# Attention value products: a head pair's thirty products in two visits instead of four, with the last 64 keys' values kept twice beside rows of zeros

## The chip, the core and the metric

The kernel runs on one core of a Trainium2 chip. The core has a matrix engine (TensorE, PE in the profile; its weight loads are listed apart as PEld), VectorE (DVE), ScalarE (ACT), GpSimd (POOL), and SyncE (SP), which issues most of the DMA transfers. Each engine works through its own queue in order. The metric is the time of one execution on the device, in microseconds; smaller is better. A profiled execution leaves a trace with the start and duration of each instruction.

## What is computed

Eight heads of four batches attend over 576 positions with 64 features per head, after rotary embedding of queries and keys. The result goes through two feed-forward layers with different nonlinearities. Everything is float32.

```python
q_rot, k_rot = rotate(q), rotate(k)                  # 4 x 8 x 576 x 64
scores = matmul(q_rot, k_rot.T) / sqrt(64)           # 576 x 576 per head
attn = exp(scores - max(scores))
attn = attn / (sum(attn) + 1e-9)
x = matmul(attn, v)                                  # heads side by side: 2304 x 512
h = x @ w_in;  x = where(h > 0, h, exp(min(h, 0)) - 1) @ w_out     # first layer
h = x @ w2_in; out = (h - tanh(h)) @ w2_out                        # second layer
```

## The kernel before

Two heads are treated together as a pair; there are 16 pairs. The 576 queries of a head are cut into four blocks of 128 and one of 64; the two blocks of 64 of a pair are put together into one. So a pair has nine **items**: item 0 is the first block of head 0, item 1 the first block of head 1, and so on to item 8, which holds the last 64 queries of both heads.

An item passes through these steps. TensorE makes its scores (`emit_s`, tile `s`, 128 queries by 576 keys; the records of line 212). VectorE takes the row maximum (`emit_max`, line 221). ScalarE takes the exponential with that maximum as bias and adds up the denominator (`emit_exp`, line 235). VectorE inverts the denominators and GpSimd scales both heads' rows (`emit_norm`, lines 248 to 252). TensorE transposes the scaled rows, 128 keys at a time (`emit_t`, tiles `pt` and `pr`, lines 292, 298 and 305). VectorE or ScalarE copies the transposes to SBUF (`flush`, lines 266 and 268), and TensorE multiplies them with the values (`emit_pv`, tile `o`, line 326). ScalarE copies `o` out (line 273).

The value products are grouped by queries: group 0 holds query blocks 0 and 1 (256 columns), group 1 blocks 2 and 3 (256 columns), group 2 the last 64 queries. Each group sums over five chunks of keys, `c` from 0 to 4, and over two heads. Chunks 0 to 3 have 128 keys each: 128 rows of the array and 64 columns. Chunk 4 has the last 64 keys, and both heads' chunks lie in one tile: head 0 in partitions 0 to 63, head 1 in 64 to 127. Their product is made with 64 rows and 64 columns. A float32 value product stands as two records in the trace.

The order is written out by hand in one loop over passes `i`. A pass issues, on TensorE, the scores of item `i+1`, then the transposes of item `i-4`, then the value products that are due; on VectorE the maximum of item `i`, the copies of the transposes made in the pass before, the inverses for item `i-1`, and pieces of the rotary embedding and of the conversion of weights; on ScalarE the exponential of item `i`, copies, and pieces of the same. When value products are due is told by `PV_AT`: for each group and chunk, how many passes after the group's last transposes. A **visit** is one pass in which TensorE makes value products. Counted from a pair's first item, they come in passes 8, 10, 12 and 14. Since pass `i` begins with the scores of item `i+1`, the text below counts **steps**: step r is the time on TensorE from the scores of item r of a pair to those of the next item. Passes 8, 10, 12 and 14 are steps 0 and 2 (of the next pair's count), 4 and 6.

Two tiles hold scores (`ps_s`, `bufs=2`), so the scores of item `n+2` wait for the exponential of item `n`. Three tiles hold transposes, one holds `o`. The keys of a pair are prepared by VectorE (the last piece, line 157, in the pass of item 4 of the pair before) and spread by four DMA transfers that SyncE issues (line 179). The values of a pair are loaded by one DMA (line 134), ten passes before their first use, into one of two tiles. After attention, TensorE does the two layers (lines 448 to 733).

The prediction speaks of the line `PV_AT`, of `load_v` and `emit_pv`, and of the tile `fm`, which holds temporaries of the conversion of weights and of both layers.

Of the kernel before, what the change touches and what calls it, by code (L numbers as in the profile page):

```python
# [8 lines left out]
F32 = mybir.dt.float32  # L9
# [14 lines left out]
def attention_elu_tanhshrink(ctx: ExitStack, tc: tile.TileContext, qk, v, w1i, w1o, w2i, w2o, tab, out):  # L24
# [6 lines left out]
    nc = tc.nc  # L31
    NPAIR = qk.shape[0]
    NTOK, DM = out.shape
    S = 576
    NB = 384
# [6 lines left out]
    const = ctx.enter_context(tc.tile_pool(name="const", bufs=1))  # L42
# [1 line left out]
    xa = const.tile([128, KC * NTOK], F32, name="xa")  # L44
    blk = {i: const.tile([128, 2, 2, NB], F32R, name=f"blk{i}") for i in range(2)}
    wmem = [const.tile([128, 8192], F32R, name="wa")]
    fm = const.tile([128, 6656], F32, name="fm")

    def x_hl(t, part, c):
        return blk[2 * t + c // 2][:, part, c % 2, :]  # L50
# [39 lines left out]
    def split_w(hi, lo, f):  # L90
        nc.scalar.copy(out=hi, in_=f)  # L91
        nc.gpsimd.tensor_tensor(out=lo, in0=f, in1=hi.bitcast(F32), op=ALU.subtract)  # L92
# [16 lines left out]
    with ExitStack() as actx:  # L109
        acst = actx.enter_context(tc.tile_pool(name="acst", bufs=1))  # L110
        p1 = actx.enter_context(tc.tile_pool(name="p1", bufs=1))
        p2 = actx.enter_context(tc.tile_pool(name="p2", bufs=2))
# [9 lines left out]
        qa_t = [acst.tile([128, 640], F32R, name=f"qa{i}") for i in range(2)]  # L122
        qb_t = [acst.tile([128, 640], F32R, name=f"qb{i}") for i in range(2)]

        t_t, hl_t, v_t, k_t = {}, {}, {}, {}

        def load_qk(p, x):
# [2 lines left out]
            t_t[p, x] = t  # L130

        def load_v(p):
            t = p2.tile([128, S], F32, tag="v", name="v")
            nc.sync.dma_start(out=t, in_=v[p])
            v_t[p] = t

        def prep(p, x, i):
            t = t_t[p, x]
# [171 lines left out]
        def emit_pv(p, grp, c):  # L310
            aT, aTr = aT_t[p, grp]
            n = 256 if grp < 2 else 64
            vt = v_t[p]

            if c == 0 and grp < 2:
                o_t[p, grp] = ps_v.tile([128, 512], F32, tag="o", name="o")
            o = o_t[p, min(grp, 1)]
            if grp == 2:
                o = o[:, 256:320]
            for h in range(2):  # L320
                sl = slice(64 * h, 64 * h + 64)
                if c < 4:
                    w, m = vt[:, 128 * c + 64 * h:128 * c + 64 * h + 64], aT[:, h, c, 0:n]
                else:
                    w, m = vt[sl, 512:576], aTr[sl, 0:n]
                nc.tensor.matmul(out=o[sl, 0:n], lhsT=w, rhs=m, start=(c == 0), stop=(c == 4))  # L326
            if c < 4:
                return
            aT_t.pop((p, grp))
            if grp == 2:  # L330
                v_t.pop(p)
            if grp != 1:
                late_x.append((p, min(grp, 1), o_t.pop((p, min(grp, 1))), 256 if grp == 0 else 320))
# [18 lines left out]
        with tc.manual_schedule():  # L352
            for x in range(2):
                t = t_t[0, x] = p2.tile([128, 2, S], F32, tag=f"t{x}", name=f"t{x}")
# [4 lines left out]
            load_qk(1, 0)  # L359
            load_qk(1, 1)  # L360
            load_v(0)
            make_identity(nc, ident)
            nc.vector.memset(zero, 0.0)
            for i in range(2):
                nc.scalar.copy(out=qa_t[i][:, S:640], in_=zero)
                nc.scalar.copy(out=qb_t[i][:, 0:64], in_=zero)
            for i in range(3):
                prep(0, 0, i)
            for i in range(3):
                prep(0, 1, i)  # L370
            n = len(items)
            pend = []
            nw = list(range(len(first_w)))[::-1]
            emit_s(0)
            PV_AT = ((1, 1, 1, 3, 3), (1, 1, 1, 3, 3), (2, 2, 2, 2, 2))
            for i in range(3, 5):
                for x in range(2):
                    prep(0, x, i)
            for i in range(n + D + 1):
                p, r = divmod(i, NI)  # L380
# [22 lines left out]
                if 0 <= i - D < n:  # L403
                    emit_t(i - D)
                    pp, uu, hh = items[i - D]
                    if uu in (1, 3) and hh == 1 or uu == 4:
                        for c in range(5):
                            pend.append((i + PV_AT[uu // 2][c], pp, uu // 2, c))
                for x in [x for x in pend if x[0] <= i]:
                    emit_pv(*x[1:])  # L410
                    pend.remove(x)
                if n - 8 <= i < n and (i - n) % 2 == 0:
                    split_x(0, (i - n + 8) // 2)
            while pend:
                emit_pv(*pend.pop(0)[1:])
# [3 lines left out]
    fcst = ctx.enter_context(tc.tile_pool(name="fcst", bufs=1))  # L419
# [6 lines left out]
    for i in range(2, 2 * NT):  # L426
        blk[i] = fcst.tile([128, 2, 2, NB], F32R, name=f"blk{i}")
    wmem.append(fcst.tile([128, 8192], F32R, name="wb"))
    gt3 = fcst.tile([128, 3, 2, NB], F32R, name="gt3")
    acc = xa  # L430
    b1 = fcst.tile([128, 1], F32, name="b1")
# [6 lines left out]
    n = len(steps)  # L438
# [13 lines left out]
        h_t[i] = hp  # L452

    def emit_act(i):
        f = fm[:, 5376 + NB * (i % 3):5376 + NB * (i % 3) + NB]
        nc.scalar.activation(out=f, in_=h_t[i], func=AF.Relu, scale=-1.0)  # L456
        nc.scalar.activation(out=f, in_=f, func=AF.Exp, scale=-1.0)
        f_t[i] = f
# [62 lines left out]
    nst, staged = [0], []  # L521

    def stage_out(cols, dst):
        st = fm[:, 4352 + 512 * (nst[0] % 2):4864 + 512 * (nst[0] % 2)][:, 0:cols.stop - cols.start]
        nst[0] += 1
        split_w(st.bitcast(F32R), GM[:, cols].bitcast(F32R), GM[:, cols])
        staged.append((dst, st, GM[:, cols]))
# [54 lines left out]
    def x2(t, k):  # L582
        return xa.rearrange("p (c n) -> p c n", n=NTOK)[:, 2 * k:2 * k + 2, NB * t:NB * t + NB]

    tms = [fm[:, o:o + 2 * NB].rearrange("p (a n) -> p a n", a=2) for o in (0, 5760, 5760)]
    XORD = ("B11", "B21", "T2", "T1", "T3", "T4", "B22")
    xb = {(tp, nm): blk[(7 * tp + k) % 8] for tp in range(NT // 2) for k, nm in enumerate(XORD)}

# [43 lines left out]
    def tmp(tag, bufs):  # L632
        base = {"s": 0, "h22": 6, "u": 7, "w": 9, "mask": 11, "f": 13}[tag]
        k = tmp_n.get(tag, 0)
        tmp_n[tag] = k + 1
        o = NB * (base + k % bufs)
        return fm[:, o:o + NB]

    LAG = 4
    with tc.manual_schedule():  # L640
# [146 lines left out]
        for q in range(nq + 1):  # L787
            live = q < nq
            p = q - 1
# [19 lines left out]
            if live:  # L809
                b, c, a, spare = banks  # L810
# [125 lines left out]
```

## Time and profile before

| | us |
|---|---|
| three runs, lowest, median, highest | 1108.22, 1108.41, 1108.49 |
| the profiled execution, its own time | 1107.93 |
| span of its trace | 1106.1 |
| TensorE busy in it | 1067.5 |
| fourteen head pairs, pair 1's first scores to pair 15's | 254.57 |

The span runs from the first instruction to the last; 1.8 us of the execution lie around it. Attention takes up the first 318 us. An engine's busy time is the time in which one of its instructions was under way, and TensorE's instructions overlap: the end of one is modelled and lies after the start of the next. So how long a group of TensorE records really holds the engine is read from start to start, not from the durations.

### The profile page before, as it was taken

The page shows a single profiled execution, that of the slowest core. Times are in us where ns is not written, and L with a number is a line of the kernel's source. Part 1 is how long each engine was busy: PE and PEld are TensorE (multiplying, and loading weights), DVE is VectorE, ACT ScalarE, POOL GpSimd, SP SyncE. Part 2 cuts the span into 40 slices and gives each one's busy share as a digit, 9 for nine tenths or more (in the row PEclk, how much of TensorE's full clock was granted, in tenths as well). Part 3 has the DMA queues.
Part 4 walks back from the last instruction along what each step waited for, and adds up shares of the span by engine and source line. Part 5 has one row for each costly group of instructions (what it writes and reads, how often), then busy time and mean ns, then how long its engine had stood idle before and what let it go on. Part 6 is the DMA issues. An engine that isn't in the chain of part 4 may idle for free.

```text
span 1106.1 us, 18779 instructions
## 1 busy us (share of the span) xinstructions
PE 1067.5 (97%) x6512; PEld 955.2 (86%) x6512; DVE 756.5 (68%) x1435; ACT 725.5 (66%) x1562; POOL 695.8 (63%) x648
## 2 busy tenths in 40 slices
PE   2999999999999999999999999999999999999998
PEld 1777776777779999999999999988998989888986
DVE  6888888888735555675766765376767667865674
ACT  2676766676757765555555555588777876878672
POOL 2877887888549766555465565556576556655552
PEclk9999999999999999999999999999999999999999
DMA  7777676767304354344443764255446754556431
GB/s 235 220 202 192 182 206 186 200 179 221 80 20 143 100 179 140 106 153 168 134 137 103 251 224 147 93 191 184 165 161 212 259 187 168 191 156 231 173 127 57
DMA packets 83390, 184.27 MB, mean 167 GB/s; under 512 B 8032, under 2 KB 43872, under 8 KB 83296
## 3 DMA queue, kind: packets, MB, share of 16 engines
q1 hardware_dynamic: 75520, 154.76, 44.2%
q10 hardware_dynamic: 7776, 28.32, 8.7%
q8 instruction: 52, 0.85, 0.3%
q14 instruction: 42, 0.34, 0.1%
HBM read 126.94 MB, written 27.79 MB: 140 GB/s over the span
## 4 chain that ended last, share of the span: by engine, by line
PE 78%; DVE 8%; POOL 5%; ACT 4%; DMA 2%; issue 2%; SPq 0%; ACTq 0%; POOLq 0%; DVEq 0%
PE y L505 18%; PE h L448 18%; PE yb L698 14%; PE hb L733 8%; PE o L326 7%; PE s L212 5%; PE pt L292 3%; PE cvb L733 3%; DVE nm L221 2%; POOL a L252 1%; ACT a L235 1%; DVE fm L766 1%; DVE t L149 1%; DMA v<-in_v 1%; DMA t<-in_qk 1%
## 5 line engine op out<-in xcount | busy, mean ns | idle before, releaser
L252 POOL TENSOR_SCALAR a<-a,r 128x576 f32<-128x576 f32 x144 | 135.6, 954 | 63.2 <-DVE r L249 43.2
L489 POOL TENSOR_TENSOR gt<-fm,gt 128x384 fp32r<-128x384 f32 x119 | 123.4, 1037 | 76.5 <-ACT gt L488 68.8
L235 ACT ACTIVATE a<-s,nm 128x576 f32<-128x576 f32 x144 | 107.0, 743 | 89.0 <-DVE nm L221 74.7
L698 PE MATMUL yb<-wb,blk 128*128 128x512 f32 x603 | 154.3, 392 | 0.4 <-POOL blk L489 0.4
L733 PE MATMUL hb<-blk,wa 128*128 128x384 f32 x720 | 139.9, 337 | 2.0 <-DVE fm L766 2.0
L221 DVE TENSOR_REDUCE nm<-s 128x1 f32<-128x576 f32 x144 | 108.2, 753 | 38.2 <-PE s L212 36.6
L733 PEld LDWEIGHTS hb<-blk,wa 128*128 128x128 f32 x720 | 127.1, 188 | 7.3 <-DVE fm L766 3.0
L698 PEld LDWEIGHTS yb<-wb,blk 128*128 128x128 f32 x603 | 112.5, 188 | 22.6 <-POOL blk L489 0.8
L456 ACT ACTIVATE fm<-h 128x384 f32<-128x384 f32 x96 | 47.3, 493 | 124.8 <-PE h L448 108.0
L489 POOL TENSOR_TENSOR blk<-fm,blk 128x384 fp32r<-128x384 f32 x67 | 71.3, 1065 | 87.8 <-ACT blk L488 59.4
L448 PE MATMUL h<-blk,wa 128*128 128x384 f32 x576 | 107.8, 335 | 0.8 <-POOL blk L55 0.6
L505 PE MATMUL y<-gt,wa 128*128 128x384 f32 x576 | 107.6, 334 | 0.1
L505 PE MATMUL y<-gt,wb 128*128 128x384 f32 x576 | 107.6, 334 | 0.0
L448 PE MATMUL h<-blk,wb 128*128 128x384 f32 x576 | 107.6, 334 | 0.0
L473 DVE TENSOR_SCALAR cvb<-fm 128x512 f32<-128x512 f32 x56 | 38.9, 694 | 98.6 <-ACT fm L471 96.0
L448 PEld LDWEIGHTS h<-blk,wa 128*128 128x128 f32 x576 | 100.3, 188 | 1.8 <-POOL blk L55 0.9
L505 PEld LDWEIGHTS y<-gt,wa 128*128 128x128 f32 x576 | 100.5, 188 | 0.4 <-issue 0.4
L505 PEld LDWEIGHTS y<-gt,wb 128*128 128x128 f32 x576 | 100.5, 188 | 0.0
L448 PEld LDWEIGHTS h<-blk,wb 128*128 128x128 f32 x576 | 100.5, 188 | 0.0
L92 POOL TENSOR_TENSOR fm<-fm 128x512 fp32r<-128x512 f32 (+1 forms) x48 | 58.4, 1220 | 57.0 <-ACT fm L91 55.8
L326 PE MATMUL o<-aT,v 128*64 128x256 f32 (+1 forms) x768 | 89.6, 338 | 2.8 <-ACT aT L268 2.4
L147 POOL TENSOR_TENSOR t<-t,tabs 128x576 f32<-128x576 f32 x59 | 86.2, 1462 | 7.9 <-DMA t<-in_qk 7.9
(124 smaller groups left out, 2281.5 us busy)
## 6 DMA issues: line engine op xcount, KB each, us to landing
wa<-wi SPq DMA_DIRECT2D x96, 448.0 KB, 5.1
wb<-wo SPq DMA_DIRECT2D x48, 512.0 KB, 6.3
k<-hl SPq DMA_DIRECT2D x64, 288.0 KB, 4.4
t<-in_qk SPq DMA_DIRECT2D x30, 576.0 KB, 6.1
wi<-fm SPq DMA_DIRECT2D x48, 256.0 KB, 2.0
fm<-in_w2o ACTq DMA_DIRECT2D x16, 512.0 KB, 3.8
wo<-fm SPq DMA_DIRECT2D x32, 256.0 KB, 3.2
fm<-in_w2i ACTq DMA_DIRECT2D x14, 512.0 KB, 3.6
```

The lines of the kernel that those rows point to most:

```text
L92: nc.gpsimd.tensor_tensor(out=lo, in0=f, in1=hi.bitcast(F32), op=ALU.subtract)
L147: eng.tensor_tensor(out=t[:, i, :], in0=t[:, i, :], in1=tabs[:, i, :], op=ALU.mult)
L212: nc.tensor.matmul(out=s[:, half, o0:o0 + n], lhsT=w, rhs=k[:, part, c0:c0 + n], start=(m == 0 and part == 0), stop=(m == len(terms) - 1 a ...
L221: nc.vector.tensor_reduce(out=nm, in_=s_t[i][:, :, 0:288], axis=AX.XY, op=ALU.max, negate=True)
L235: nc.scalar.activation(out=a.rearrange("p (x c) -> p x c", x=2), in_=s[:, :, 0:288], func=AF.Exp, bias=nm_t.pop(i), scale=1.0, accum_out=den,)
L252: nc.gpsimd.tensor_scalar(out=a, in0=a, scalar1=r[:, x:x + 1], scalar2=1.0, op0=ALU.mult, op1=ALU.mult)
L326: nc.tensor.matmul(out=o[sl, 0:n], lhsT=w, rhs=m, start=(c == 0), stop=(c == 4))
L448: nc.tensor.matmul(out=hp, lhsT=w[:, wp, ws], rhs=x_hl(t, xp, c), start=(m == 0), stop=(m == 3 * KC - 1))
L489: nc.gpsimd.tensor_tensor(out=g[:, 1, :], in0=f, in1=g[:, 0, :].bitcast(F32), op=ALU.subtract)
L505: nc.tensor.matmul(out=y_t[e][:, 0:NB], lhsT=w[:, wp, es], rhs=gt[:, gp, :], start=st, stop=sp)
L698: nc.tensor.matmul(out=y, lhsT=gt[:, gp, es], rhs=w[:, wp, :], start=(j == 0 and k == 0), stop=(j == NJ - 1 and k == 2))
L733: nc.tensor.matmul(out=bank, lhsT=w[:, wp, o:o + 128], rhs=x[:, xp, cc, :], start=(start and k == 0), stop=(stop and k == 5), skip_group_c ...
```

## The change

All thirty value products of a pair are now made in two visits, in passes 9 and 14 (steps 1 and 6): group 0 two passes after its last transposes, group 1 three, group 2 two. Chunk 4 is made in the same shape as the others, 128 rows by 64 columns: the values of the last 64 keys are loaded twice side by side, head 0's in columns 512 to 575 with zeros in the lower 64 partitions, head 1's in columns 576 to 639 with zeros in the upper 64. The zeros are written once, at the start. The value tiles become two fixed tiles of 640 columns, and a pair's values are loaded by three DMAs instead of one. Part of `fm` moves to a new tile `fn`, allocated after attention; only the two layers use it, and their instructions and their order stay as they were.

```diff
-    fm = const.tile([128, 6656], F32, name="fm")
+    fm = const.tile([128, 4352], F32, name="fm")
...
+        vt_t = [acst.tile([128, 640], F32, name=f"v{i}") for i in range(2)]
...
         def load_v(p):
-            t = p2.tile([128, S], F32, tag="v", name="v")
-            nc.sync.dma_start(out=t, in_=v[p])
-            v_t[p] = t
+            t = v_t[p] = vt_t[p % 2]
+            nc.sync.dma_start(out=t[:, 0:512], in_=v[p, :, 0:512])
+            for h in range(2):
+                sl = slice(64 * h, 64 * h + 64)
+                nc.sync.dma_start(out=t[sl, 512 + 64 * h:576 + 64 * h], in_=v[p, sl, 512:576])
...
                 if c < 4:
                     w, m = vt[:, 128 * c + 64 * h:128 * c + 64 * h + 64], aT[:, h, c, 0:n]
                 else:
-                    w, m = vt[sl, 512:576], aTr[sl, 0:n]
+                    w, m = vt[:, 512 + 64 * h:576 + 64 * h], aTr[:, 0:n]
                 nc.tensor.matmul(out=o[sl, 0:n], lhsT=w, rhs=m, start=(c == 0), stop=(c == 4))
...
+                nc.gpsimd.memset(vt_t[i][64:128, 512:576], 0.0)
+                nc.gpsimd.memset(vt_t[i][0:64, 576:640], 0.0)
...
-            PV_AT = ((1, 1, 1, 3, 3), (1, 1, 1, 3, 3), (2, 2, 2, 2, 2))
+            PV_AT = ((2, 2, 2, 2, 2), (3, 3, 3, 3, 3), (2, 2, 2, 2, 2))
...
+    fn = fcst.tile([128, 2304], F32, name="fn")
...
     def emit_act(i):
-        f = fm[:, 5376 + NB * (i % 3):5376 + NB * (i % 3) + NB]
+        f = fn[:, 1024 + NB * (i % 3):1024 + NB * (i % 3) + NB]
...
-        st = fm[:, 4352 + 512 * (nst[0] % 2):4864 + 512 * (nst[0] % 2)][:, 0:cols.stop - cols.start]
+        st = fn[:, 512 * (nst[0] % 2):512 * (nst[0] % 2) + 512][:, 0:cols.stop - cols.start]
...
-        o = NB * (base + k % bufs)
-        return fm[:, o:o + NB]
+        o = base + k % bufs
+        m, o = (fm, NB * o) if o < 11 else (fn, NB * (o - 11))
+        return m[:, o:o + NB]
```

On TensorE, at the visits of groups 1 and 2 of the first pair (`a` with a number is item 8's tile, `aT` the transposes of chunks 0 to 3, `aTr` those of chunk 4, `k`, `qa` and `qb` the keys and queries), before:

```order
L292 MATMUL pt<-ident,a_316 128x128 x4
L298 MATMUL pr<-ident,a_316 64x64 x2
L326 MATMUL o<-aT,v 64x256 x6
L212 MATMUL s<-k_193,qb_93 128x288 x4
L292 MATMUL pt<-ident,a 128x128 x4
L212 MATMUL s<-k_190,qa_91 128x288 x4
L292 MATMUL pt<-ident,a 128x128 x4
L305 MATMUL pr<-ident,a 128x128
L326 MATMUL o<-aT,v 64x256 x2
L326 MATMUL o<-aTr,v 64x256 x2
L326 MATMUL o<-aT_433,v 64x64 x8
L326 MATMUL o<-aTr_434,v 64x64 x2
```

And now:

```order
L295 MATMUL pt<-ident,a_324 128x128 x4
L301 MATMUL pr<-ident,a_324 64x64 x2
L215 MATMUL s<-k_200,qb_93 128x288 x4
L295 MATMUL pt<-ident,a 128x128 x4
L215 MATMUL s<-k_197,qa_91 128x288 x4
L295 MATMUL pt<-ident,a 128x128 x4
L308 MATMUL pr<-ident,a 128x128
L329 MATMUL o<-aT,v_94 64x256 x8
L329 MATMUL o<-aTr,v_94 64x256 x2
L329 MATMUL o<-aT_441,v_94 64x64 x8
L329 MATMUL o<-aTr_442,v_94 64x64 x2
```

The six products that followed item 8's transposes have gone to the later visit, and the 64-row shape is left in line 301 alone. On TensorE, at the visits of group 0 of the second pair, before:

```order
L292 MATMUL pt<-ident,a 128x128 x4
L326 MATMUL o<-aT,v 64x256 x6
L212 MATMUL s<-k_472,qb_92 128x288 x4
L292 MATMUL pt<-ident,a 128x128 x4
L305 MATMUL pr<-ident,a 128x128
L212 MATMUL s<-k_469,qa_90 128x288 x4
L292 MATMUL pt<-ident,a 128x128 x4
L326 MATMUL o<-aT,v 64x256 x2
L326 MATMUL o<-aTr,v 64x256 x2
```

And now:

```order
L295 MATMUL pt<-ident,a 128x128 x4
L215 MATMUL s<-k_473,qb_92 128x288 x4
L295 MATMUL pt<-ident,a 128x128 x4
L308 MATMUL pr<-ident,a 128x128
L329 MATMUL o<-aT,v_95 64x256 x8
L329 MATMUL o<-aTr,v_95 64x256 x2
```

Here ten products stand together, one pass after the place where six of them stood.

## Rows read from the trace of the kernel before

**Rows 1.** Windows of fourteen head pairs: length, then engines' busy time, sum and mean.

```profile
sum 254.57, PE 247.78 PEld 187.76 DVE 215.43 ACT 176.47 POOL 205.98; mean PE 17.70 PEld 13.41 DVE 15.39 ACT 12.61 POOL 14.71
```

**Rows 2.** Timeline of TensorE, one head pair: start, duration, what (records) [idle before].

```profile
108.55 0.80 PE L212 MATMUL s<-k,qa 128*128 128x288 f32 x4 [0.16 <-ACT a L235]
...
109.72 1.52 PE L326 MATMUL o<-aT,v 128*64 128x256 f32 x12
111.16 0.79 PE L212 MATMUL s<-k,qb 128*128 128x288 f32 x4
...
113.64 0.65 PE L326 MATMUL o<-aT,v 128*64 128x256 f32 x4
114.22 0.65 PE L326 MATMUL o<-aTr,v 64*64 64x256 f32 x4
114.80 0.79 PE L212 MATMUL s<-k,qb 128*128 128x288 f32 x4
...
115.92 0.80 PE L212 MATMUL s<-k,qa 128*128 128x288 f32 x4
...
119.38 0.80 PE L212 MATMUL s<-k,qb 128*128 128x288 f32 x4
...
120.37 0.77 PE L212 MATMUL s<-k,qa 128*128 128x288 f32 x4
...
122.78 0.69 PE L326 MATMUL o<-aT,v 128*64 128x64 f32 x16
123.39 0.33 PE L326 MATMUL o<-aTr,v 64*64 64x64 f32 x4
123.66 0.80 PE L212 MATMUL s<-k,qb 128*128 128x288 f32 x4
...
124.65 0.77 PE L212 MATMUL s<-k,qa 128*128 128x288 f32 x4
...
126.41 0.38 PE L212 MATMUL s<-k,qa 128*128 128x288 f32 x1
```

**Rows 3.** Timeline of weight loads at one visit.

```profile
109.72 1.06 PEld L326 LDWEIGHTS o<-aT,v 128*64 128x64 f32 x12 [0.17 <-issue]
```

**Rows 4.** Groups of TensorE, shapes apart: busy us, mean ns | idle before.

```profile
L326 PE MATMUL o<-aT,v 128*64 128x256 f32 x512 | 78.6, 393 | 2.8 <-ACT aT L268 2.4
...
L326 PE MATMUL o<-aTr,v 64*64 64x256 f32 x128 | 20.8, 402 | 0.0
```

**Rows 5.** Waits over twelve pairs: who for whom, us in total, times, longest.

```profile
ACT a L235 <- DVE nm L221: 53.6, 58, 1.8
...
DVE nm L221 <- PE s L212: 22.7, 41, 1.6
...
PEld o L326 <- ACT aT L268: 7.4, 12, 1.9
PEld pr L298 <- ACT aT L268: 3.7, 3, 1.4
```

**Rows 6.** Groups over the same twelve pairs: busy us, mean ns | idle before.

```profile
L221 DVE TENSOR_REDUCE nm<-s 128x1 f32<-128x576 f32 x109 | 81.8, 753 | 24.0 <-PE s L212 22.7
L235 ACT ACTIVATE a<-s,nm 128x576 f32<-128x576 f32 x108 | 80.3, 744 | 65.9 <-DVE nm L221 53.6 <-DVE den L248 9.9 <-PE o L326 1.5
...
L235 ACT ACTIVATION_READ_ACCUMULATOR a<-s,nm 128x1 f32 x108 | 21.4, 198 | 0.0
```

**Rows 7.** Timeline of SyncE's queue behind one pair's keys.

```profile
120.46 3.42 SPq L179 DMA_DIRECT2D k<-hl  x4
123.98 1.25 SPq L134 DMA_DIRECT2D v<-in_v  x1
```

**Rows 8.** The key copies' line: durations of issuing, and time to landing.

```profile
L179 SPq DMA_DIRECT2D k<-hl x48: 461/680/1502, 65.4 to 268.1; - x48
...
DMA to landing us min/median/max: 3.0/4.5/7.1
```

**Rows 9.** Timeline of GpSimd at the start.

```profile
7.47 1.40 POOL L147 TENSOR_TENSOR t<-t,tabs 128x576 f32<-128x576 f32 x1 [6.18 <-DMA t<-in_qk]
```

More of the change, by code (lines that the diff above doesn't have):

```diff
@@ L583, in x2 @@
         return xa.rearrange("p (c n) -> p c n", n=NTOK)[:, 2 * k:2 * k + 2, NB * t:NB * t + NB]
-    tms = [fm[:, o:o + 2 * NB].rearrange("p (a n) -> p a n", a=2) for o in (0, 5760, 5760)]
+    tms = [m[:, o:o + 2 * NB].rearrange("p (a n) -> p a n", a=2) for m, o in ((fm, 0), (fn, 1536), (fn, 1536))]
     XORD = ("B11", "B21", "T2", "T1", "T3", "T4", "B22")
```

## The prediction, made before the changed kernel ran

> **What bounds the kernel now.** I read the windows, pair by pair, first. Fourteen head pairs take 254.57 us, 18.18 each, and in each TensorE is busy 17.70 us, VectorE 15.39, GpSimd 14.71, ScalarE 12.61 [rows 1]. The reader is to see that TensorE leads, but that VectorE stands only 2.8 us behind it, so that a saving on TensorE can't be worth more than about that per pair.
>
> Then the timeline of TensorE in one pair, from start to start, since its ends are modelled [rows 2]. A step without a visit takes 0.99 us (119.38 to 120.37), or 1.12 with the extra transpose of chunk 4 (114.80 to 115.92); step 8 takes 1.76. The visits' steps take 2.61, 3.46 and 3.29 (steps 0, 4 and 6). The inside of a visit tells more. Twelve records of 128 rows and 256 columns go from 109.72 to the next scores at 111.16, 1.44 us. Four of them go from 113.64 to 114.22, 0.58 us, before the shape changes. Eight more records cost 0.86, so 0.1075 each; four cost 0.43, and 0.15 is left. That 0.15 is paid where the shape of the array's use changes. The four 64-row records after them take 0.58 again (114.22 to 114.80): the same 0.43 and the same 0.15. Of the 64-column records, sixteen take 0.61 (122.78 to 123.39) and four 0.27 (123.39 to 123.66): 0.028 each and 0.16 for the change. So I count changes of shape: between 128x128 (scores, transposes), 128x64 (chunks 0 to 3) and 64x64 (chunk 4, and item 8's small transpose).
>
> Last the waits. Twelve pairs hold 7.4 us in which value products, and 3.7 in which the small transposes among them, wait for ScalarE's copies: 0.93 per pair [rows 5]. They come because three chunks are due one pass after the transposes, and need copies of that very pass, which ScalarE makes behind an exponential. On the other side VectorE waits 22.7 us for scores, 1.9 per pair, and ScalarE 53.6 for maxima [rows 5]. TensorE and the ring scores, maximum, exponential wait for each other in turn.
>
> **The change, part by part.** *Changes of shape.* Before, a pair has 13: two around step 0's visit, three at step 2, three at step 4 with the small transpose ahead of it, five at step 6. After, it has 6: two for each visit and two for the small transpose, which now stands alone. Seven go, 7 x 0.15 = 1.05 us per pair on TensorE.
>
> *Chunk 4 with 128 rows.* The products are as many as before, and a record's length is 393 ns in the one shape and 402 in the other [rows 4], with 0.58 us for four from start to start in both. I take nothing. From the nearest rows the bounds are a 9 ns gain per record, 12 records a pair, 0.1 us, and as much lost.
>
> *Waits for copies.* The products now stand at least one pass behind the copies they need, so the 0.93 goes where it stands. What is late next is the ring: the scores of item n+2 wait for the exponential of item n, and VectorE has to make the maxima. So I follow one pair after the change. VectorE's 15.39 us make 1.71 per step: 0.71 to the end of the maximum, 1.0 of other work behind it. The exponential takes 0.74, the read of its sum 0.20 [rows 6], so it is through 0.92 us after the maximum, overlaps taken off. Scores have landed 0.8 after their first record starts [rows 2]. The steps of TensorE by themselves: step 1 is 1.12 + 20 x 0.1075 + 0.30 = 3.57; step 6 is 1.12 + 2.15 + 20 x 0.028 + 0.30 = 4.13; step 4, with the small transpose, 0.99 + 0.11 + 0.30 = 1.40; the others as above. They add up to 15.9.
>
> Zero is where item 6's scores are issued, the second visit behind them. Maximum 5 runs 0.1 to 0.8, maximum 6 1.8 to 2.5, and VectorE is through at 3.5. Scores 7 are issued at 4.1 and landed at 4.9: VectorE idles 1.4. Maximum 7 ends at 5.6, scores 8 are issued at 5.1, maximum 8 ends at 7.35, and scores 9 are issued at 6.9. Scores 10 would be due at 7.9 but wait for exponential 8, at 8.3. The first visit follows, and scores 11 are issued at 11.8; VectorE, through at 11.8, idles until 12.6. Scores 12 come at 12.8, scores 13 at 14.3 (exponential 11), scores 14 at 16.0 (exponential 12), scores 15 at 17.7 (exponential 13). The period is 17.7 us: VectorE's 15.4 and 2.3 of idling in front of the two visits' scores.
>
> The same walk with the steps of before, and with 0.8 for each of the two waits for a copy (ScalarE's exponential and copy of some 0.6 end that much behind the transposes), comes to 18.5, where 18.18 was measured. So it is 0.3 too long, and I take 17.4 after the change: 0.8 us less per pair. Over the fourteen pairs that is 11 us, and at the end of the last pair, where no scores are left to wait for, the 1.05 comes in full: 12 us. The bounds for the part: if the ring never waited, 15.9 against 18.18 is 2.2 per pair, 32 us; if the ring gave everything back, nothing.
>
> *The loads of values.* One DMA becomes three. SyncE spends up to 1.25 us on one [rows 7], so up to 2.5 more per pair. Behind it stand a load of the next queries or keys and the spreading of queries, which SyncE gets to late anyway. The values are in place a whole pair before their use, which hides a longer landing. The keys' four DMAs stand ahead of it and are not held back. I take nothing; were the next load of queries late by the whole 2.5 us, GpSimd would lose some 1 us a pair of its 3.5 us of idle time.
>
> *Start.* Four memsets of 64 x 64 on GpSimd lie in the 6.18 us in which it waits for the first load [rows 9]. Even at 1.40 us each, what its multiplication of a whole 128 x 576 tile takes [rows 9], they would make 5.6 and fit; without that cover 5.6 is the most they could cost. *The tile `fn`.* Same instructions in the same order on all engines; its first writer comes behind the last value products anyway. Nothing.
>
> The profiled execution is 1107.93, its span 1106.1; the median of the runs is 0.5 above it. 1107.9 - 12 + 0.5 is 1096.
>
> **A rule against it.** Weight loads and products overlap in the rows: at the first visit twelve weight loads of 1.06 us in all lie inside the 1.44 us of the twelve products [rows 2, 3], though all use the same 128 rows. The Trainium skill says otherwise (TensorE: Matmul & The Clock Gate, Part 3: Packing small matmuls): a weight load overlaps products in flight only when it goes to another group of rows. By that rule the 64-row chunks of before, whose two heads use different rows, hide their loads, and the new 128-row ones don't. The trace does not bear it out; I give it little, as a rival.
>
> **The rivals.** *Scores stand behind long visits.* At steps 1 and 6 scores now stand behind twenty and forty records, where VectorE had at most 3.46 + 0.8 us to bridge, now 4.1 + 0.8. My walk gives VectorE two steps of work, 3.4 us, for each visit. It decides where VectorE's idle time passes 2.8 us per pair, the 18.18 less 15.39 of now. If it finds two thirds of a step less to do at the two visits together, 1.1 us, the period is 17.4 + 1.1 = 18.5, 0.3 longer than now, and 14 x 0.3 - 1 = 3 us are lost: 1111. For it speaks that VectorE already waits 1.9 for scores; against it, that the two steps behind a visit are short and let it run at its own pace.
>
> *The keys come late.* Scores 10 need the last of four key DMAs, issued as VectorE ends its preparation at about 0.1 on my clock. The four take 3.42 us to issue [rows 7], and one lands 4.5 us after its issue, at most 7.1 [rows 8]; the last is issued some 2 us in, so it lands 6.5 to 9.1 after the first issue, against the 8.2 left. At 9.1 scores 10 come 0.9 late and so does the pair. The saving is gone then; at half of that 0.4 per pair is left, 1107.9 - 6 - 1 + 0.5 = 1102. Before, these scores stood 2.61 us or more behind the scores of item 9 (step 0), now 1.4 by my walk.
>
> *TensorE alone decides.* If VectorE's share of overlaps and its lighter passes let it keep step, the period nears 15.9 to 16.5: 24 to 32 us less, 1077 to 1085.
>
> *The weight loads show* (the rule's case): four records of chunk 4 per group, three groups, 12 loads of 0.088 us (1.06 / 12) [rows 3] are 1.06 us a pair, as much as the saving on shapes. The value products then gain nothing, and with the longer visits it goes as in the first rival: 1111.
>
> **How the numbers follow.** The forecast, 1096 within 1090 to 1101, gets 0.50. TensorE alone, below 1090, 0.15. The keys late or VectorE's idling half grown, 1101 to 1106, 0.16. The two balanced, no change, 0.09. The long visits, 1111, 0.08, and the weight loads, 0.02. Faster than before by over 0.2% (2.2 us, about what a measurement of this kernel can tell from no change), that is under 1106.2: 0.81. Within it 0.09, slower 0.10. A range from 1084 to 1108 leaves out about 0.05 below and 0.15 above.
>
> **What would show it.** In the profile after: 64x64 records left in line 301 alone; four 128-row records of chunk 4 in 0.43 us, without 0.15 before them; no wait of value products for ScalarE's copies; the period from pair to pair at 17.4; TensorE idle before scores, ended by ScalarE's exponentials; VectorE idle before the maxima of items 7 and 11, some 1 us each. The layers as long as before. I am wrong if TensorE waits for the keys' DMAs, if VectorE's idle time passes 2.8 us per pair, or if the 128-row chunk 4 is longer than the 64-row one.

## The result, and the profile after

The changed kernel is slower: a median of 1118.62 us (1118.44 to 1120.14, four runs) against 1108.45 for the kernel before on the same chip, a ratio of 1.0095 with a 95% interval of 1.0078 to 1.0113. The forecast was 1096 within 1084 to 1108, so both the sign and the range missed. The profiled execution took 1120.14, with a span of 1118.0; it is the slowest of the four, so the traces lie some 2 us further apart than the medians. In this profile `emit_s` is line 215, the maximum 224, the exponential 238, and the value products 329.

First the windows of the same fourteen pairs (stretch and its length; busy time, with instructions, of PE, PEld, DVE, ACT and POOL; granted clock, DMA share, GB/s), which answer to [rows 1]:

```profile
130.82:149.42 18.60, 16.75 (x149) 13.67 (x148) 15.21 (x36) 12.82 (x33) 14.66 (x14) 1.00 0.73 189
...
168.13:190.45 22.32, 18.31 (x150) 14.68 (x148) 16.37 (x37) 12.48 (x33) 14.04 (x14) 0.92 0.64 164
...
sum 266.96, PE 238.19 PEld 193.52 DVE 214.86 ACT 176.87 POOL 206.18; mean PE 17.01 PEld 13.82 DVE 15.35 ACT 12.63 POOL 14.73
```

The pairs take 12.39 us more. Around them the first pair starts 0.50 later, and the time from pair 15's first scores to the first layer falls from 28.14 to 27.29: 12.0, against 11.9 between the spans. So the loss lies in the pairs. TensorE is busy 0.69 less per pair, VectorE as long as before, and both stand idle more.

Then the timeline of TensorE in pair 6 (start, duration, what, [idle before and what ended it]), which answers to [rows 2]:

```profile
130.82 0.77 PE L215 MATMUL s<-k,qa 128*128 128x288 f32 x4
...
132.71 0.77 PE L215 MATMUL s<-k,qb 128*128 128x288 f32 x4 [0.69 <-ACT a L238]
...
133.96 1.95 PE L329 MATMUL o<-aT,v 128*64 128x256 f32 x16
135.74 0.60 PE L329 MATMUL o<-aTr,v 128*64 128x256 f32 x4
136.27 0.80 PE L215 MATMUL s<-k,qa 128*128 128x288 f32 x4
...
137.27 0.78 PE L215 MATMUL s<-k,qb 128*128 128x288 f32 x4
...
138.85 0.80 PE L215 MATMUL s<-k,qa 128*128 128x288 f32 x4 [0.26 <-ACT a L238]
...
140.45 0.80 PE L215 MATMUL s<-k,qb 128*128 128x288 f32 x4
...
142.49 0.81 PE L215 MATMUL s<-k,qa 128*128 128x288 f32 x4 [0.80 <-ACT a L238]
...
146.67 0.80 PE L215 MATMUL s<-k,qb 128*128 128x288 f32 x4
```

The visits are what the prediction made them: step 1 from 132.71 to 136.27 takes 3.56 (forecast 3.57), step 6 from 142.49 to 146.67 takes 4.18 (4.13). The four records of chunk 4 follow the sixteen without a gap. What is new is at the right: scores that wait. The view names an exponential for all three rows. For 138.85 and 142.49 that holds: they start 0.14 us after the exponential has ended. For 132.71, item 1's scores, it does not. Here are the issue of the pair's last key transfer and the exponential that freed the score tile, from the timelines of SyncE and ScalarE:

```profile
127.69 0.83 SPq L182 DMA_DIRECT2D k<-hl  x1
...
131.62 0.74 ACT L238 ACTIVATE a<-s,nm 128x576 f32<-128x576 f32 x1
```

The exponential was through at 132.36, 0.35 us earlier; the transfer took 4.83 us to land, until 132.52, and the scores start 0.20 after that. So these waited for the keys.

The waits say how much (who for whom, us in total, times, longest; twelve pairs, as in [rows 5]). After the change:

```profile
DVE nm L224 <- PE s L215: 32.2, 26, 2.6
...
PEld s L215 <- ACT a L238: 24.4, 40, 1.3
...
PEld pr L301 <- ACT aT L271: 5.0, 3, 1.7
```

In the same view of the kernel before, scores waited for exponentials like this:

```profile
PEld s L212 <- ACT a L235: 2.3, 7, 0.4
```

No value product waits for a copy any more, where 7.4 us stood [rows 5]. But the weight loads of scores wait 24.4 us for exponentials, 2.0 per pair, where they waited 2.3 in all. (Of the 24.4, 0.9 is the wait at 132.71 above.) VectorE's idle time before maxima has grown from 22.7 to 32.2, in fewer and longer pieces. Here is the longest piece of pair 6, in VectorE's timeline:

```profile
133.53 0.76 DVE L224 TENSOR_REDUCE nm<-s 128x1 f32<-128x576 f32 x1
134.20 0.68 DVE L269 COPY aT<-pt 128x512 f32<-128x512 f32 x1
137.11 0.76 DVE L224 TENSOR_REDUCE nm<-s 128x1 f32<-128x576 f32 x1 [2.23 <-PE s L215]
```

The exponential behind that maximum, in ScalarE's timeline:

```profile
137.97 0.74 ACT L238 ACTIVATE a<-s,nm 128x576 f32<-128x576 f32 x1 [1.20 <-DVE den L251]
```

VectorE is through at 134.88 and idles until the scores issued at 136.27 have landed. Maximum, exponential and the next scores but one (138.85) then follow one by one: 2.58 us for steps 2 and 3, and while that runs it is TensorE that idles.

### The profile page after: what moved, and what is told of

The parts are those of the page before. It is cut to its first block, busy times and chain, and to the rows that moved or that the text cites. A ratio compares the mean times of both kernels' runs of the same rounds, so it can differ in the third digit from the quotient of the medians.

```text
span 1118.0 us, 18846 instructions
## 1 busy us (share of the span) xinstructions
PE 1054.7 (94%) x6512; PEld 960.2 (86%) x6512; DVE 756.2 (68%) x1435; ACT 726.5 (65%) x1562; POOL 697.0 (62%) x652
## 4 chain that ended last, share of the span: by engine, by line
PE 73%; DVE 10%; POOL 6%; ACT 6%; issue 3%; DMA 2%; SPq 1%; ACTq 0%; POOLq 0%; DVEq 0%
PE y L511 18%; PE h L454 17%; PE yb L705 14%; PE hb L740 8%; PE o L329 6%; PE s L215 4%; PE cvb L740 3%; DVE nm L224 3%; ACT a L238 2%; PE pt L295 2%; DVE t L152 1%; POOL a L255 1%; DMA v<-in_v 1%; DVE fn L773 1%; POOL t L150 1%
## 5 line engine op out<-in xcount | busy, mean ns | idle before, releaser
L495 POOL TENSOR_TENSOR gt<-fn,gt 128x384 fp32r<-128x384 f32 x119 | 123.4, 1037 | 77.1 <-ACT gt L494 69.5
L705 PEld LDWEIGHTS yb<-wb,blk 128*128 128x128 f32 x603 | 112.5, 188 | 22.7 <-POOL blk L495 0.8
L462 ACT ACTIVATE fn<-h 128x384 f32<-128x384 f32 x96 | 47.3, 492 | 125.1 <-PE h L454 108.5
L495 POOL TENSOR_TENSOR blk<-fn,blk 128x384 fp32r<-128x384 f32 x67 | 71.3, 1065 | 87.8 <-ACT blk L494 59.4
L92 POOL TENSOR_TENSOR fm<-fm,fn 128x512 fp32r<-128x512 f32 (+1 forms) x48 | 58.3, 1219 | 56.5 <-ACT fn L91 55.3
L295 PE MATMUL pt<-ident,a 128*128 128x128 f32 x576 | 88.5, 277 | 0.1
```

The lines of the kernel that those rows point to most:

```text
L295: nc.tensor.transpose(pt[:, c, :], a[:, h or 0, c0:c0 + 128], ident)
L495: nc.gpsimd.tensor_tensor(out=g[:, 1, :], in0=f, in1=g[:, 0, :].bitcast(F32), op=ALU.subtract)
L705: nc.tensor.matmul(out=y, lhsT=gt[:, gp, es], rhs=w[:, wp, :], start=(j == 0 and k == 0), stop=(j == NJ - 1 and k == 2))
```

## The experiments

Each was timed beside the kernel before, whose median then was 1107.65 to 1108.45; ratios are to it, with 95% intervals. The table gives the mean length of the steps of pairs 1 to 14, worked out from the starts of scores in each profile's timeline of TensorE, their sum as `pair` (up to 0.01 off by the rounding), and the time in which weight loads of scores waited for exponentials in twelve pairs (2 to 13), from the view of waits.

| kernel | us | step 0 | 1 | 2 | 3 | 4 | 5 | 6 | 7 | 8 | pair | waits |
|---|---|---|---|---|---|---|---|---|---|---|---|---|
| before | 1108.4 | 3.20 | 1.15 | 2.31 | 1.10 | 3.31 | 0.99 | 3.29 | 1.01 | 1.82 | 18.18 | 2.3 |
| after | 1118.6 | 1.96 | 3.60 | 0.99 | 1.58 | 2.01 | 1.81 | 4.28 | 0.99 | 1.84 | 19.06 | 24.4 |
| e1_visits | 1126.3 | 1.70 | 3.72 | 1.00 | 1.58 | 2.01 | 1.84 | 4.78 | 0.99 | 1.77 | 19.38 | 25.3 |
| e2_padding | 1100.5 | 3.15 | 1.15 | 2.16 | 1.11 | 3.30 | 0.99 | 2.85 | 1.08 | 1.90 | 17.70 | 3.8 |
| e3_four_late | 1105.9 | 1.95 | 2.70 | 1.14 | 2.28 | 1.57 | 2.61 | 1.23 | 2.75 | 1.78 | 18.02 | 9.2 |
| e4_three | 1119.2 | 2.11 | 3.68 | 1.01 | 1.56 | 3.59 | 0.99 | 2.85 | 1.10 | 1.95 | 18.85 | 17.9 |
| e7_first_split | 1107.9 | 3.32 | 1.15 | 2.16 | 1.11 | 1.72 | 1.81 | 4.17 | 0.99 | 1.76 | 18.19 | 11.1 |
| e8_pass_ten | 1116.5 | 1.92 | 1.96 | 3.50 | 1.10 | 1.57 | 1.82 | 4.17 | 0.99 | 1.76 | 18.78 | 31.1 |
| e11_after_keys | 1117.5 | 1.74 | 3.58 | 1.11 | 1.66 | 2.02 | 1.76 | 4.24 | 0.99 | 1.79 | 18.89 | 32.3 |
| e14_padding_keys | 1110.5 | 3.13 | 1.16 | 2.24 | 1.36 | 3.49 | 1.09 | 2.85 | 1.10 | 1.94 | 18.36 | 10.8 |
| e5_before_nomax | 1091.0 | 2.66 | 1.11 | 2.30 | 1.10 | 2.85 | 0.99 | 3.29 | 0.99 | 1.76 | 17.05 | 0.8 |
| e6_after_nomax | 1094.1 | 1.86 | 3.55 | 0.99 | 1.08 | 1.52 | 1.50 | 4.16 | 0.99 | 1.77 | 17.44 | 10.8 |
| e9_before_light | 1088.0 | 2.76 | 1.11 | 2.30 | 1.10 | 2.85 | 0.99 | 3.29 | 0.99 | 1.76 | 17.15 | 0.8 |
| e13_before_light_keys | 1090.1 | 2.73 | 1.11 | 2.30 | 1.10 | 2.99 | 0.99 | 3.29 | 0.99 | 1.76 | 17.26 | 0.8 |
| e10_after_light | 1090.2 | 1.64 | 3.61 | 0.99 | 1.08 | 1.46 | 1.54 | 4.17 | 0.99 | 1.77 | 17.25 | 8.6 |
| e12_light_keys | 1082.0 | 1.06 | 3.61 | 0.99 | 1.08 | 1.73 | 1.36 | 4.16 | 0.99 | 1.76 | 16.73 | 7.0 |

### Which of the two parts

e1_visits is the kernel before with the new visits alone, and e2_padding the changed kernel with the old visits:

```diff
-            PV_AT = ((1, 1, 1, 3, 3), (1, 1, 1, 3, 3), (2, 2, 2, 2, 2))    # e1_visits
+            PV_AT = ((2, 2, 2, 2, 2), (3, 3, 3, 3, 3), (2, 2, 2, 2, 2))
...
-            PV_AT = ((2, 2, 2, 2, 2), (3, 3, 3, 3, 3), (2, 2, 2, 2, 2))    # e2_padding
+            PV_AT = ((1, 1, 1, 3, 3), (1, 1, 1, 3, 3), (2, 2, 2, 2, 2))
```

> The kernel before with the two-visit table alone; chunk 4 stays 64x64, one load of values. Theory A (scores stand behind long visits, and TensorE then waits for the ring of maximum and exponential, about 1.7 us more per pair than before): as slow as the changed kernel or slower, since a pair keeps 10 changes of shape instead of 6 (4 x 0.15 x 16 = 9.6 us more, part of it hidden in the waits): 1119 to 1128. Theory B (the padded chunk 4 and its three loads cost the time): like before or faster, 1103 to 1109.

> The changed kernel with the old table: four visits in passes 8, 10, 12 and 14, chunk 4 padded to 128 rows, three loads. Four changes of shape go per pair, 0.6 us. Theory A: faster than before, up to 9.6 us, part of it lost to waits for copies: 1099 to 1106. Theory B: slower than before, 1112 to 1120.

e1_visits took 1126.27, 1.0165 [1.0148, 1.0182]; e2_padding 1100.49, 0.9934 [0.9919, 0.9949]. The two parts pull apart: the visits cost 18.4 us by themselves, the padding saves 7.4. Theory A's ranges hold in both. Up to some 5 of the 18.4 may be the clock's: in the profiled execution of e1_visits TensorE ran at half clock for three stretches of 3.4 us (from 33.8, 85.0 and 184.0). e2_padding beats both kernels. In it the padding is seen by itself: step 2 is 0.15 shorter and step 6 0.44, one and three changes of shape fewer, and no price of the 64 rows of zeros shows.

### Which visit

Four other tables in the changed kernel. e3_four_late keeps four visits, each one pass later; e4_three brings group 0 together and leaves the rest as before; e7_first_split leaves group 0 as before and brings groups 1 and 2 together; e8_pass_ten is the change with the first visit a pass later.

```diff
-            PV_AT = ((2, 2, 2, 2, 2), (3, 3, 3, 3, 3), (2, 2, 2, 2, 2))
+            PV_AT = ((2, 2, 2, 4, 4), (2, 2, 2, 4, 4), (3, 3, 3, 3, 3))    # e3_four_late
...
+            PV_AT = ((2, 2, 2, 2, 2), (1, 1, 1, 3, 3), (2, 2, 2, 2, 2))    # e4_three
...
+            PV_AT = ((1, 1, 1, 3, 3), (3, 3, 3, 3, 3), (2, 2, 2, 2, 2))    # e7_first_split
...
+            PV_AT = ((3, 3, 3, 3, 3), (3, 3, 3, 3, 3), (2, 2, 2, 2, 2))    # e8_pass_ten
```

> The changed kernel with four visits, one pass later than in the old table (passes 9, 11, 13 and 15, the last with group 2), so that no product needs a copy of its own pass. Theory A: faster than the padding with the old table by up to the 0.93 us per pair of waits for copies, less what the ring takes: 1094 to 1103. Theory B: slower than before, 1112 to 1120.

> The changed kernel with three visits: group 0 whole in pass 9, group 1 in passes 12 (chunks 0 to 2) and 14 (the rest, with group 2). Theory A: one long visit less; between the padding with the old table and the changed kernel, 1102 to 1112. Theory B: slower than before like the changed kernel, 1114 to 1120.

> The changed kernel with three visits: group 0 as in the old table, passes 8 and 10, groups 1 and 2 whole in pass 14. Theory A1 (it is the visit in pass 9 that hurts, since VectorE has little to do in passes 9 and 10; it idles 1.65 us there per pair): 1098 to 1106. Theory A2 (each long visit hurts by its length, the one in pass 14 the more, being the longest): 1110 to 1119.

> The changed kernel with group 0's whole visit one pass later, passes 10 and 14; both visits as long as in the changed kernel. Theory A1: VectorE has an inverse and an addition of the rotary embedding in pass 11 to do behind that visit, some 1.2 us more than in pass 10, so its idle time falls by about as much per pair: 1100 to 1108. Theory A2: same length, same cost, 1115 to 1122.

| | us | ratio | over e2_padding |
|---|---|---|---|
| e3_four_late | 1105.87 | 0.9983 [0.9974, 0.9992] | 5.4 |
| e4_three | 1119.17 | 1.0105 [1.0088, 1.0123] | 18.7 |
| e7_first_split | 1107.89 | 1.0001 [0.9992, 1.0011] | 7.4 |
| e8_pass_ten | 1116.52 | 1.0078 [1.0063, 1.0093] | 16.0 |

Bringing products together costs at either visit, and most at the first: 18.7 for group 0 alone, 7.4 for groups 1 and 2 alone, 18.1 for both, so the two don't add. e8_pass_ten shows that it isn't only the first visit's pass: there the waits for exponentials grow to 31.1, and only 2.1 us come back, within the two intervals. With four visits one pass later 5.4 are lost. That need not be the price of lateness: no visit stands in step 0 there, and in five of the fourteen pairs the scores of item 1 wait for the last key transfer, and start 6.9 us later in all than 0.14 us after the exponential that they need.

Several expectations missed. e3_four_late came out above theory A's range and e4_three above it too, in theory B's, which e2_padding had already ruled out. e7_first_split lies between A1 and A2; e8_pass_ten is in A2's range.

### What holds the scores: the ring

In e5_before_nomax and e6_after_nomax a constant zero column takes the place of the row maximum, in the kernel before and in the changed one. In e9_before_light and e10_after_light VectorE also makes the rotary multiplications that GpSimd had.

```diff
-            nm = sm.tile([128, 1], F32, tag="nm", name="nm")
-            nc.vector.tensor_reduce(out=nm, in_=s_t[i][:, :, 0:288], axis=AX.XY, op=ALU.max, negate=True)
-            nm_t[i] = nm
+            nm_t[i] = zero[:, 0:1]
...
-                    eng = nc.vector if p < 2 and i == 1 else nc.gpsimd    # e9, e10 only
+                    eng = nc.vector
```

> The kernel before without the row maximum: the exponential takes zero as its bias, so VectorE loses 0.75 us per item and the ring from scores to scores has one engine less (for these inputs the result is the same, the scores being small). Theory A (TensorE waits for the ring through VectorE): the pair's period falls from 18.18 towards TensorE's own 17.0: 1088 to 1098. Theory C (the long visits cost by something outside the ring, as the granted clock or transfers): 1100 to 1108.

> The changed kernel without the row maximum, else as the run before. Theory A: the period falls from 19.06 to 16.0 to 16.6, TensorE's own, and the change turns into a gain of 10 to 17 us against the same edit on the kernel before: 1073 to 1085. Theory C: it stays some 10 us slower than the same edit on the kernel before.

> The kernel before without the row maximum, and with all multiplications of the rotary embedding on VectorE instead of GpSimd, so that no engine but TensorE is near its limit (VectorE some 12 us per pair, GpSimd 9, ScalarE 12.6). TensorE is at its own pace already without the maximum (period 17.05), so every theory has it there: 1088 to 1093.

> The changed kernel with the same two edits. Theory A (long visits cost because the engines that feed TensorE are nearly full and two score tiles let them work ahead by two items only; without the maximum GpSimd was the next of them): the period falls from 17.44 to about 16.2, and the kernel is 10 to 16 us faster than the same edits on the kernel before: 1073 to 1082. Theory C (something in the long visits themselves): no faster than the same edits on the kernel before, 1088 to 1095.

e5_before_nomax took 1091.04, 0.9846 [0.9831, 0.9860], and e6_after_nomax 1094.10, 0.9870 [0.9855, 0.9884]: the gap between the kernels falls from 10.2 to 3.1. With step 3 it is plainest: 1.58 in every pair of the changed kernel, 1.08 without the maximum. But the changed kernel stayed the slower one, between the ranges of A and C, and in e6_after_nomax something else came late (its waits, twelve pairs):

```profile
DVE t L152 <- POOL t L150: 30.2, 19, 3.5
```

VectorE there waits for GpSimd's multiplications, a wait that the maxima had covered. e9 and e10 take that away: 1088.03, 0.9822 [0.9807, 0.9836], and 1090.19, 0.9848 [0.9832, 0.9865]. The gap is still 2.2: theory A missed, and theory C's range holds. In the table step 0 stands out: 1.64 in the mean of e10_after_light, but 0.96 in three of its pairs. TensorE's timeline there at pair 6:

```profile
118.21 0.77 PE L215 MATMUL s<-k,qa 128*128 128x288 f32 x4
118.81 0.60 PE L293 MATMUL pt<-ident,a 128*128 128x128 f32 x4
119.53 0.77 PE L215 MATMUL s<-k,qb 128*128 128x288 f32 x4
```

And the view of the tile `k` for that pair's last two key transfers (durations of issuing, start of the first and the last; below it the time to landing):

```profile
L182 SPq DMA_DIRECT2D k<-hl x2: 1117/1169/1221, 113.1 to 114.4; - x2
...
DMA to landing us min/median/max: 4.9/4.9/5.0
```

The last transfer, issued at 114.4, lands at 119.3, and the scores that read it start at 119.53. Over the pairs 2 to 15 these scores start 0.14 to 0.28 us after the landing in 12 of 14. In the changed kernel it is 0.20 to 0.29 in 7 of 14, in the kernel before in one. So the keys were a second suspect.

### The keys

Four kernels bring the preparation of the keys one pass forward: e11 is the changed kernel with that edit, e12 and e13 are e10 and e9 with it, e14 is e2_padding with it.

```diff
-                when = [i0 + o for o in ((-10, -6, -4, -3, -2, -1), (-7, -2, 0, 2, 3, 4))[x]]
+                when = [i0 + o for o in ((-10, -6, -4, -3, -2, -1), (-8, -3, -1, 1, 2, 3))[x]]
```

> The changed kernel, with the five steps of preparation of a pair's key (load, two multiplications, addition, rounding, remainder and the four transfers) each one pass earlier; the visits stay in passes 9 and 14. In the changed kernel the scores of item 1 start 0.19 to 0.29 us after the last key transfer lands in 7 of 14 pairs, and 0.5 to 1.6 us after it in the others. Theory K (keys late at step 0, beside the ring of maximum, exponential and scores): step 0 falls from 1.96 us by some 0.3 to 0.5 us in the mean, since the maximum of item 0 is the next thing that the scores wait for: 1112 to 1116 us. Theory R (only the ring of VectorE and TensorE holds the scores): within 2 us of the changed kernel, 1117 to 1121. The other steps should stay within 0.2 us of theirs by both.

> The changed kernel without the row maximum (a constant zero column takes its place, which leaves that part of the computation out) and with all rotary multiplications on VectorE, with the key's preparation one pass earlier. Without that edit it took 1090.2 us, and the scores of item 1 started 0.14 to 0.28 us after the last key transfer in 12 of 14 pairs. Theory K: step 0 falls from 1.64 us to 1.0 to 1.2, 6 to 9 us in 14 pairs: 1081 to 1085, then 3 to 7 us under the kernel before in the same form (1088.0), and most of what the saved changes of shape should give comes out. Theory without K: what holds step 0 is TensorE's own work or the ring, and the time stays at 1088 to 1092.

> The control: the kernel before without the row maximum and with all rotary multiplications on VectorE, with the key's preparation one pass earlier. There the scores of item 1 start 0.6 to 2.4 us after the last key transfer, since the first visit of the pair before stands ahead of them in step 0. Theory K expects no gain: 1087 to 1089 us, as without the edit (1088.0). If it gains more than 2 us too, the edit does something else than bring the keys in time.

> The padding alone (visits in four passes), with the key's preparation one pass earlier. Without that edit it took 1100.5 us; the scores of item 1 start 0.2 to 3.4 us after the last key transfer, under 0.45 us in 3 of 14 pairs. Theory K: little to gain, 0 to 2 us: 1098 to 1101. If the preparation's VectorE work in other passes lengthens the ring there, 1101 to 1104.

e12_light_keys took 1082.01, 0.9765 [0.9750, 0.9779], 8.2 less than e10_after_light, as theory K had it: step 0 falls to 1.06, and in pair 6 the scores of item 1 now start 0.96 behind those of item 0:

```profile
117.69 0.77 PE L215 MATMUL s<-k,qa 128*128 128x288 f32 x4
118.30 0.60 PE L293 MATMUL pt<-ident,a 128*128 128x128 f32 x4
118.65 0.79 PE L215 MATMUL s<-k,qb 128*128 128x288 f32 x4
```

The control, e13_before_light_keys, took 1090.13, 0.9837 [0.9823, 0.9852]: no gain, 2.1 lost, 1 us beyond what was expected. With the maximum gone and the keys in time the change turns into a gain, 6.0 us on e9_before_light and 8.1 on the control. The windows of the fourteen pairs, in e12_light_keys:

```profile
sum 234.33, PE 226.59 PEld 190.21 DVE 162.41 ACT 174.97 POOL 154.98; mean PE 16.18 PEld 13.59 DVE 11.60 ACT 12.50 POOL 11.07
```

And in the control:

```profile
sum 241.74, PE 239.32 PEld 186.72 DVE 160.65 ACT 177.19 POOL 147.28; mean PE 17.09 PEld 13.34 DVE 11.47 ACT 12.66 POOL 10.52
```

TensorE is busy 0.91 less per pair, and the pairs take 7.4 less together: here about half of the 1.1 us per pair comes out at the end. The rest is left in the exponentials, for which the scores still wait 7.0 us in twelve pairs.

In the changed kernel itself the same edit brings next to nothing: e11_after_keys took 1117.47, 1.0082 [1.0067, 1.0097], 1.1 less than the changed kernel. Theory K missed there and R held. Its waits, in twelve pairs:

```profile
PEld s L215 <- ACT a L238: 32.3, 44, 1.9
...
DVE nm L224 <- PE s L215: 14.2, 23, 1.4
```

The scores that had waited for keys now wait for exponentials instead, 32.3 where 24.4 stood: item 1's start 0.14 us after an exponential's end in 13 of 14 pairs, where that was so in 7. The keys are late in the changed kernel, but the ring stands right behind them.

e14_padding_keys took 1110.51, 1.0024 [1.0014, 1.0033], 10 us more than e2_padding and a miss by both expectations. The five pieces of the key's preparation, on GpSimd, VectorE and ScalarE, fall into other passes there, steps 2 to 5 grow by 0.6 us together, and the waits for exponentials from 3.8 to 10.8. So in this kernel the place of these pieces, with the same work, is worth 10 us. Which of them it is was not tried; and in e11_after_keys the same price may hide a gain.

## Why the prediction was wrong

*TensorE's own terms were right.* Seven changes of shape less at 0.15 were put at 1.05 us per pair, and TensorE's bare steps at 15.9. The shortest length of each step over the fourteen pairs, added up, is 16.94 in the kernel before and 15.84 in e12_light_keys: 1.10 less. Chunk 4 with 128 rows was put at nothing between 0.1 of gain and loss:

```profile
L329 PE MATMUL o<-aT,v 128*64 128x256 f32 x512 | 63.0, 389 | 0.0
...
L329 PE MATMUL o<-aTr,v 128*64 128x256 f32 x128 | 19.2, 379 | 0.0
```

That is the groups' view, busy us and mean ns; [rows 4] had 393 and 402. The weight loads do not show, so the rival with the smallest chance fell. At the first visit of pair 6 the view of weight loads has

```profile
133.96 1.49 PEld L329 LDWEIGHTS o<-aT,v 128*64 128x64 f32 x16 [0.17 <-issue]
```

which lie inside the 1.78 us of their products (133.96 to 135.74), though all use the same 128 rows. The Trainium skill (TensorE: Matmul & The Clock Gate, Part 3: Packing small matmuls) has a line by which loads overlap products in flight only in another group of rows, though the same section also lets a load into the background weight buffer be pulled ahead. This trace does not agree with that line, and e2_padding, faster by 7.4 us with all its value products in 128 rows, doesn't either.

*The waits for copies went*, as predicted, at the value products. At the small transposes they stayed, 5.0 us where 3.7 stood.

*No cost of the loads or the start shows*, as predicted: e2_padding has them too, and the last key transfer of a pair lands 5.4 us after its issue (median of pairs 1 to 15) in the kernel before and in the changed one. SyncE spends 1.29 and 1.87 us on a pair's values, behind the keys:

```profile
125.11 3.41 SPq L182 DMA_DIRECT2D k<-hl  x4
128.62 1.29 SPq L135 DMA_DIRECT2D v<-in_v  x1
130.01 1.87 SPq L138 DMA_DIRECT2D v<-in_v  x2
```

Before they were 3.42 for the keys and 1.25 for the values [rows 7]. Each of the four memsets on GpSimd took a tenth of its bound, in the wait for the first load, as [rows 9] had room for:

```profile
1.35 0.15 POOL L370 MEMSET v<- 64x64 f32 x1
```

*The walk of the ring failed.* It gave VectorE "1.71 per step", the same in each, and came to 17.7, corrected to 17.4; 19.06 was measured. It had the two steps behind the first visit right (2.58 against 2.5), and the visits too. Step by step it was short at step 0 (1.4, measured 1.96) and at steps 4 and 5 (1.71 each, 2.01 and 1.81). VectorE's pieces don't lie evenly: at the first visit of pair 6 it has one copy left behind its maximum and is through 1.39 us before the next scores are issued, where the walk had it through as they were. Over the pair VectorE's time outside its work is 19.06 - 15.35 = 3.7 us, where the walk had 2.3. The correction of -0.3, taken from the same walk through the kernel before, went the wrong way too: the evenly loaded walk came out too long for the four visits and too short for the two.

The walk also left ScalarE's other work at nothing: it had each exponential through 0.92 us behind its maximum. In pair 6, in the timelines of VectorE and ScalarE, item 4 went like this:

```profile
140.05 0.75 DVE L224 TENSOR_REDUCE nm<-s 128x1 f32<-128x576 f32 x1
...
140.45 0.69 ACT L155 ACTIVATE hl<-t 128x576 fp32r<-128x576 f32 x1
...
141.03 0.68 ACT L74 ACTIVATE fm<-fm 128x512 f32<-128x512 f32 x1
...
141.60 0.74 ACT L238 ACTIVATE a<-s,nm 128x576 f32<-128x576 f32 x1
```

The maximum ends at 140.80, and ScalarE rounds the next pair's keys and takes a step of the conversion of weights before it turns to the exponential. Over the pairs 1 to 14 this exponential starts 0.35 to 1.87 us after its maximum has ended, 1.03 in the mean, and the scores of item 6 wait for it in all fourteen. In the kernel before it was 0.91, but there the visit in step 4 covered it. With the maximum left out these scores still wait for an exponential in all fourteen pairs of e10_after_light. No run moves ScalarE's pieces by themselves, so their share of the loss stays open.

Step by step, then. At step 0 the walk missed both VectorE's pieces (1.71 in the mean of the seven pairs in which an exponential ends the wait) and the keys (2.27 in the six in which they do). At step 4 it was right in eleven pairs (1.76 in the mean); in the other three, 2.9 each, the small transposes wait for ScalarE's copy, a wait that the prediction had among the 0.93 that go. At step 5 the size was nearly right, but the wait is for ScalarE.

The sum per pair, as the runs have it: TensorE's bare steps 1.1 less, as forecast. Time above them: 18.18 - 16.94 = 1.2 before and 19.06 - 15.84 = 3.2 after, 2.0 more. Of these 1.8 are the added waits of scores for exponentials ((24.4 - 2.3) / 12). Two stretches at half clock (below) are some 0.2. The keys hold item 1's scores in six of the fourteen pairs, which start 5.9 us later in all than 0.14 us after the exponential they need, 0.4 per pair, of which e11_after_keys gets next to nothing back. The waits for copies at the value products are 0.6 less (7.4 / 12), those at the small transposes 0.1 more. These parts add up to some 1.9 of the 2.0. So 0.9 per pair are lost, 12.4 in fourteen.

*The rivals.* "Scores stand behind long visits" was the right one: its point of decision, 2.8 us of idling per pair, is passed with 3.7. It had a chance of 0.08 and a price of 3 us where the runs show 10. Its two sides in the text, long visits against short steps behind them, were weighed by that walk. "The keys come late" was right in its mechanism, in six of fourteen pairs; taking it away alone brought 1.1 us here, and 8 where the maximum is left out. I gave both as rivals of each other, but they stand one behind the other. Two of the three signs of being wrong that the prediction named have come: TensorE waits for the keys, and VectorE idles more than 2.8 us per pair.

## What to carry to other kernels

A saving on the engine that leads is worth its size only where the work on the next engine can be spread over the new gaps: before work is put together, list for the longest new gap what the other engine has left to do in its queue order, piece by piece, not by a mean per step; and for the short steps behind it, what stands ahead of each link of the ring on every engine, ScalarE's exponential here as much as VectorE's maximum. Split a change into its parts before it is judged: here one part saves 7 us and the other costs 18. And a wait that is taken away uncovers the one behind it, so an edit that brings nothing (keys early, 1.1 us) may still be needed by the next one (8.2 us).

## What the runs showed of the hardware

The granted clock fell to half twice in the changed kernel's attention (windows, columns as above):

```profile
35.40:38.80 3.40, 3.40 (x17) 3.38 (x16) 3.18 (x7) 2.03 (x5) 2.56 (x3) 0.50 0.96 354
...
178.00:182.00 4.00, 2.02 (x18) 1.47 (x16) 3.42 (x8) 3.45 (x9) 4.00 (x5) 1.00 0.00 0
182.20:185.60 3.40, 3.40 (x17) 2.49 (x18) 3.33 (x9) 1.02 (x3) 1.69 (x2) 0.50 0.75 153
```

In each stretch of 3.4 us TensorE ran at 1.2 GHz and was busy throughout. Ahead of the second it had been busy 2.02 of 4.00 us. In the kernel before it was at full clock in the same places, as was the whole attention of e2_padding (profiled executions). The second stretch lies in a visit, which took 5.76 us (step 6 of pair 8) instead of 4.16; the first cost pair 1 some 0.5 us in step 1 and 0.5 before. So by this estimate some 2.5 us of the loss in this execution go to the clock; 3.4, half of the two stretches, is the most it can be. Both falls came behind idle time of TensorE (the first behind 3.02 us that ended at 33.90); why other gaps left the clock alone stays open.

A change of the shape in use costs 0.15 us on TensorE, measured a second time: e2_padding saves one in step 2 (0.15) and three in step 6 (0.44).
